# Low parts behind the next slice's products, and weight roundings that start three slices later, in a gated mixing stage

## The chip, the cores and the metric

The kernel runs on one core of a Trainium2 chip. A core has five engines that run side by side: TensorE (matmuls into PSUM; PE in the profile), VectorE (DVE), ScalarE (ACT), GpSimd (POOL) and SyncE (SP, which here only issues transfers). The metric is the device time of one execution in microseconds (us). Matmuls are done in three passes of rounded operands: each fp32 operand is split into a high part (rounded to the matmul's format, `fp32r`) and a low part (what the rounding left), and high x high, high x low and low x high are summed.

## The reference

Three blocks run one after the other on 4 batches of 768 tokens, 384 features:

```
attn:  per head a delta-rule scan over 768 tokens; its output is x
moe:   h = gelu(x @ w_in);  u, v = halves of h (512 features each)
       v_n = layernorm(v) * g_ln
       v_s = einsum('ts,bsd->btd', w_sg, v_n) + b_sg      # mixing over the tokens
       x   = x + (u * v_s) @ w_out                        # gate, projection
moe2:  xk, xr = two mixes of x with x of the token before
       out = sigmoid(xr @ w_r) * (relu(xk @ w_k)**2 @ w_v)
```

The change lies in the second block's mixing, gate and projection. There the weights w_r and w_v of the third block are also split into their parts, piece by piece, and put into DRAM, to be loaded again for the third block.

## The kernel before, in words

The scan and the first half of the gate unit fill the time to about 360 us. Then comes the stage of the change. It works through eight halves (`halves`, L1037): a half is one batch b and 384 of its tokens (t = 0 or 1). Each half has four slices d of 128 features; `mix(b, t, d)` (L1046) is one slice, 32 in all, which I number 0 to 31 (slices 0 to 3 are batch 0, t = 0; 4 to 7 batch 0, t = 1, and so on).

One slice: TensorE adds up 18 matmuls in a PSUM bank (`mix_mm`, six chunks of tokens, three passes). VectorE applies the scale and the bias into `w` (L1056, reads the bank) and multiplies with u (L1058). ScalarE rounds `w` to the high part `gh` (L120 by way of `split`, L117), and VectorE takes the low part `gl` = w - gh (L123). `w` has two buffers. When the four slices of a half are there, `project` (L1064) lets TensorE run 36 matmuls with w_out (three output blocks of 12, in the order of the slices), and VectorE adds each block to x (L1072). The projection of a half t = 0 is called after the third slice of the half t = 1 (`PD`); that of a half t = 1 at the start of the next batch, after `begin` has put the first four chunks' matmuls of all four slices of the next batch before it (L1082 to L1084).

The v rows that the matmuls read stand in a ring of tiles `g` (chunk c of batch b): `fetch_v` loads them from DRAM on SP's queue, `to_ring` (L888) splits them: ScalarE rounds, and the low part is VectorE's for chunks 0 and 3 and GpSimd's for the others. Chunks 0 to 2 of the next batch are split after slice d = 1 of the half t = 1, chunks 3 to 5 after d = 3 (L1092 to L1100). `load_u` loads u two halves ahead; three buffers.

The split of a piece of w_r or w_v is a job (`narrow`, L154; eleven jobs: three of w_r, eight of w_v): a load by SP into one of three `raw` buffers, a conversion on ScalarE (L164), four instructions on VectorE (L169, L171, L173, L175), one on GpSimd (L177), then the rounding on ScalarE (L120) and the low part on GpSimd (L123), then a write to DRAM by SP (L202). `side(n)` (L1012) places the next n VectorE instructions of the open jobs at the point where it is called; `starts` (L1010) tells at which slice the three buffers first take a job. Two slices lie between a job's load and its first instruction.

The order on the four computing engines and on SP's queue is the order in which the code calls them in this stage (manual schedule). After the last slice the rest of the jobs is drained (L1101). GpSimd's queue then issues the reload of w_v (L1118) and of w_r (L1145); the third block starts with `shift`, whose work on VectorE and ScalarE a scheduler interleaves.

Of the kernel before, what the change touches and what calls it, by code (L numbers as in the profile page):

```python
# [7 lines left out]
F32 = mybir.dt.float32  # L8
# [3 lines left out]
AF = mybir.ActivationFunctionType  # L12
ALU = mybir.AluOpType
# [48 lines left out]
NRAW = 3  # L62
NNA = 2
PD = 2
SD = 1
CS = (5, 4)
VF = (0, 3)
VD = 1
# [18 lines left out]
def fused_kernel(  # L87
# [18 lines left out]
    V, A, G, T = nc.vector, nc.scalar, nc.gpsimd, nc.tensor  # L106
# [10 lines left out]
    def split(eng_hi, eng_lo, src, hi, lo):  # L117

        if eng_hi is A:
            A.activation(hi, src, AF.Copy)  # L120
        else:
            eng_hi.tensor_scalar(hi, src, 1.0, None, op0=ALU.mult)
        eng_lo.tensor_tensor(lo, src, hi.bitcast(F32), op=ALU.subtract)  # L123
# [831 lines left out]
    def mix_mm(pt, b, t, d, c):  # L955
        ds_ = slice(d * P, d * P + P)
        vh, vl = ring[b, c]
        wh, wl = wsl[t][c]
        for i, (v, w) in enumerate(((vh, wh), (vh, wl), (vl, wh))):
            T.matmul(pt[:, :DM], lhsT=v[:, ds_], rhs=w, start=(c == 0 and i == 0),  # L960
                     stop=(c == 5 and i == 2))
# [45 lines left out]
    wr_dh, wr_dl, j2 = scratch(w_r, "wr", 3, DM, DM, st)  # L1007
    wv_dh, wv_dl, j3 = scratch(w_v, "wv", 8, DM, DM, st)
    jobs += j2 + j3
    live, turns, starts = [], [0], [1 + 2 * i for i in range(NRAW)]  # L1010

    def side(n):  # L1012

        while n > 0:
            while jobs and any(x <= turns[0] for x in starts):
                starts.remove(next(x for x in starts if x <= turns[0]))
                j = jobs.pop(0)()
                next(j)
                live.append([turns[0] + 2, j, None])
            e = next((e for e in live if e[0] <= turns[0]), None)  # L1020
            if e is None:
                return
            if e[2]:
                e[2]()
            e[2] = None
            c = next(e[1], None)
            if c is None:
                live.remove(e)
                starts.append(turns[0] + 1)
            elif isinstance(c, tuple) and c[0]:  # L1030
                e[0], e[2] = turns[0] + 1, c[1]
            elif isinstance(c, tuple):
                c[1]()
            else:
                n -= 1

    halves = [(b, t) for b in range(B) for t in range(2)]  # L1037
    us, gs = {}, {}
# [7 lines left out]
    def mix(b, t, d):  # L1046
        sl = slice(t * DM, t * DM + DM)
        pt, c0 = begun.pop(d, (None, 0))
        if pt is None:
            pt = ps.tile([P, HF], F32, name="ms")  # L1050
        for c in range(c0, 6):
            mix_mm(pt, b, t, d, c)
        if d == 0:
            gs[b, t] = [mp.tile([P, 4, DM], F32R, name=x) for x in ("gh", "gl")]
        w = vr.tile([P, DM], F32, name="w", bufs=2)
        V.scalar_tensor_tensor(w, pt[:, :DM], g_sb[:, d:d + 1], b_sb[:, sl],  # L1056
                               op0=ALU.mult, op1=ALU.add)
        V.tensor_tensor(w, w, us[b, t][:, d], op=ALU.mult)  # L1058
        side(1)
        split(A, V, w, gs[b, t][0][:, d], gs[b, t][1][:, d])  # L1060
        side(SD)
        turns[0] += 1

# [13 lines left out]
    for k, (b, t) in enumerate(halves):  # L1077
# [7 lines left out]
        for d in range(4):  # L1085
            if (t, d) == VF and b + 1 < B:
                for c in range(3):
                    fetch_v(b + 1, c)
            mix(b, t, d)
            if d == (PD if k < 7 else 3) and t:  # L1090
                project(*halves[k - 1])
            if t == 1 and b + 1 < B:  # L1092
                if d == VD:
                    for c in range(3):
                        load_v(b + 1, c)
                    for c in range(3, 6):
                        fetch_v(b + 1, c)
                if d == 3:
                    for c in range(3, 6):
                        load_v(b + 1, c)  # L1100
# [136 lines left out]
```

## Time and profile before

| | us |
|---|---|
| three runs: median (lowest to highest) | 755.34 (751.11 to 757.25) |
| the profiled execution | 752.32 |
| its span | 750.3 |
| TensorE busy in the span | 690.7 (92%) |
| VectorE busy | 510.8 (68%) |
| ScalarE busy | 368.8 (49%) |
| GpSimd busy | 202.4 (27%) |

The span is what the profiler saw of one execution; 2.0 us of the execution's time lie around it. Busy shares are means over stages that differ. A wait is idle time of an engine, put down to the instruction that ended it. Times in the rows count from the span's start.

### The profile page before, as it was taken

How to read it: one execution, taken by the hardware profiler on the slowest of the kernel's cores; microseconds unless marked ns; L12 is line 12 of the kernel's file. 1: busy time of each engine (PE TensorE's matmuls, PEld its weight loads, DVE VectorE, ACT ScalarE, POOL GpSimd, SP SyncE). 2: the span in 40 equal slices, each digit the busy share in tenths (PEclk: the TensorE clock that was granted, in tenths of full speed). 3: DMA queues.
4: the chain of work that ended last, by engine and by line, in shares of the span. 5: the costliest groups of instructions: out<-in, count | busy, mean ns of one | idle time of the engine just before them, and what ended most of it. 6: DMA issues, size and time to landing. Idle time of an engine off the chain costs nothing.

```text
span 750.3 us, 24940 instructions
## 1 busy us (share of the span) xinstructions
PE 690.7 (92%) x10832; PEld 640.4 (85%) x10832; DVE 510.8 (68%) x1070; ACT 368.8 (49%) x752; POOL 202.4 (27%) x253
## 2 busy tenths in 40 slices
PE   2568789999898999899989999999999999999998
PEld 2536568878776887779989999999999999999997
DVE  6989999878988795632494949489556564563341
ACT  2226656777666666874232313148445454452240
POOL 3033534454445355453133414420000000000000
PEclk9988989999999999999999999999999999999999
DMA  8503542674555565758755454195000000000000
GB/s 249 118 30 84 140 112 81 178 207 139 147 179 152 162 179 169 223 148 240 240 175 190 127 168 148 66 278 141 33 11 21 32 12 22 22 11 31 12 22 32
DMA packets 81549, 88.75 MB, mean 118 GB/s; under 512 B 24704, under 2 KB 64320, under 8 KB 81440
## 3 DMA queue, kind: packets, MB, share of 16 engines
q1 hardware_dynamic: 76384, 77.72, 35.1%
q0 software_dynamic: 5056, 9.44, 4.6%
q8 instruction: 85, 1.39, 0.8%
q14 instruction: 24, 0.20, 0.1%
HBM read 56.60 MB, written 25.82 MB: 110 GB/s over the span
## 4 chain that ended last, share of the span: by engine, by line
PE 73%; DVE 16%; DMA 4%; issue 3%; POOL 1%; SPq 1%; ACT 1%; POOLq 0%; DVEq 0%; ACTq 0%
PE ms L151 38%; PE ms L960 11%; PE ms L687 6%; PE ms L635 5%; DVE sg L355 4%; DVE sg L393 2%; PE ms L563 2%; PE rk L521 2%; PE sps L549 2%; PE ms L456 2%; PE rk L534 1%; PE rk L498 1%; PE ms L333 1%; PE ms L726 1%; DVE Yt L393 1%
## 5 line engine op out<-in xcount | busy, mean ns | idle before, releaser
L177 POOL TENSOR_TENSOR na<-na,raw 128x256 int32<-128x256 int32 (+2 forms) x43 | 36.4, 846 | 121.6 <-DVE na L175 53.5
L151 PE MATMUL ms<-wvh,sl 128*128 128x384 f32 x192 | 64.6, 336 | 0.0
L151 PE MATMUL ms<-wvl,sh 128*128 128x384 f32 x192 | 64.5, 336 | 0.0
L151 PE MATMUL ms<-wvh,sh 128*128 128x384 f32 x192 | 64.5, 336 | 0.0
L151 PE MATMUL ms<-xm_hi,sw0h 128*128 128x384 f32 x192 | 64.2, 335 | 0.0
L151 PE MATMUL ms<-xm_hi,sw0l 128*128 128x384 f32 x192 | 64.2, 334 | 0.0
L151 PE MATMUL ms<-xm_lo,sw0h 128*128 128x384 f32 x192 | 64.2, 334 | 0.0
L120 ACT ACTIVATE gh<-w 128x384 fp32r<-128x384 f32 x32 | 16.8, 525 | 94.9 <-DVE w L1058 94.9
L123 DVE TENSOR_TENSOR sl<-sg,sh 128x384 fp32r<-128x384 f32 x64 | 35.7, 558 | 30.2 <-ACT sh L120 30.2
L960 PE MATMUL ms<-sw0h,g 128*128 128x384 f32 x192 | 50.6, 336 | 3.0 <-ACT g L120 2.1
L120 ACT ACTIVATE sh<-sg 128x384 fp32r<-128x384 f32 x64 | 33.5, 524 | 35.9 <-DVE sg L1157 35.9
L960 PE MATMUL ms<-ws1h,g 128*128 128x384 f32 x192 | 49.9, 334 | 0.0
L355 DVE TENSOR_TENSOR sg<-sg,Yt 128x512 f32<-128x512 f32 (+10 forms) x78 | 46.7, 599 | 1.8
L1173 DVE TENSOR_TENSOR sg<-sg,ms 128x384 f32<-128x384 f32 x24 | 13.3, 554 | 45.3 <-PE ms L151 45.3
L1157 DVE TENSOR_TENSOR sg<-sg 128x384 f32<-128x384 f32 x64 | 35.5, 554 | 10.9 <-ACT sg L1156 10.9
L1156 ACT ACTIVATE sg<-ms 128x384 f32<-128x384 f32 x64 | 30.8, 481 | 23.7 <-PE ms L151 22.9
L514 POOL TENSOR_SCALAR_AFFINE_SELECT SQ<-SQ 64x512 f32<-64x512 f32 x36 | 27.5, 763 | 52.9 <-ACT SQ L513 51.7
L335 PE MATMUL ms<-kT 64*32 64x64 f32 (+1 forms) x640 | 23.3, 235 | 17.9 <-issue 17.9
L687 PE MATMUL ms<-xl,wiu_hi 128*128 128x256 f32 x144 | 39.7, 297 | 0.0
L687 PE MATMUL ms<-xh,wiu_lo 128*128 128x256 f32 x144 | 38.6, 291 | 0.9 <-issue 0.9
L333 PEld LDWEIGHTS ms<-kT 64*32 64x32 f32 x640 | 20.0, 131 | 22.2 <-issue 14.5
L120 ACT ACTIVATE xm_hi<-sg 128x384 fp32r<-128x384 f32 x48 | 23.3, 516 | 31.4 <-PE ms L151 30.5
(246 smaller groups left out, 2237.8 us busy)
## 6 DMA issues: line engine op xcount, KB each, us to landing
u_d<-ug SPq DMA_DIRECT2D x24, 256.0 KB, 3.8
u<-u_d SPq DMA_DIRECT2D x16, 384.0 KB, 4.6
vn_d<-v SPq DMA_DIRECT2D x22, 256.0 KB, 2.8
vk<-in_vk_dram SPq DMA_DIRECT2D x24, 192.0 KB, 4.0
vk<-in_vk_dram SPq DMA_DIRECT2D x12, 384.0 KB, 4.8
out_dram<-sg SPq DMA_DIRECT2D x24, 192.0 KB, 1.9
kT<-in_kt_d_dram SPq DMA_DIRECT2D x8, 512.0 KB, 5.8
SQ<-in_q_d_dram SPq DMA_DIRECT2D x36, 96.0 KB, 4.1
```

The source lines that it names most:

```text
L120: A.activation(hi, src, AF.Copy)
L123: eng_lo.tensor_tensor(lo, src, hi.bitcast(F32), op=ALU.subtract)
L151: T.matmul(pt, lhsT=a, rhs=b, start=(i == 0), stop=(i == n - 1))
L177: G.tensor_tensor(a.bitcast(I32), a.bitcast(I32), w_lo.bitcast(I32), op=ALU.add)
L333: T.matmul(gps[r:r + 32, p, c0:c1], lhsT=t[r:r + 64, u, 0:32], rhs=t[r:r + 64, u, c0:c1], start=True, stop=True)
L355: V.tensor_tensor(tv, vw(a_t, a_off, a_dims), vw(b_t, b_off, b_dims), op=ALU.mult)
L514: G.affine_select(out=pt, in_=pt, pattern=[[0, 8], [1, C]], compare_op=ALU.is_gt, fill=0.0, base=0, channel_multiplier=-1)
L635: T.matmul(vstat[g, b], lhsT=a[:, c], rhs=w[:, c], start=first, stop=last)
L687: T.matmul(vstat["u"][:, 2 * P * d:2 * P * d + 2 * P], lhsT=w[:, c, ds_], rhs=a[:, c].rearrange("p b t -> p (b t)"), start=first, stop=last)
L960: T.matmul(pt[:, :DM], lhsT=v[:, ds_], rhs=w, start=(c == 0 and i == 0), stop=(c == 5 and i == 2))
L1156: A.activation(r, pt[:, :DM], AF.Relu)
L1157: V.tensor_tensor(r, r, r, op=ALU.mult)
```

## The change

Three things. The low part of a slice is no longer taken behind its own rounding but kept in a list (`owing`) and issued after the next slice's product with u; at the fourth slice of a half t = 1 both open low parts are issued. The three `raw` buffers take their first jobs at slices 4, 6 and 8 instead of 1, 3 and 5. And a slice's two job instructions both stand at its end (`SD = 2`); before, one stood ahead of the low part and one behind (at the fourth slice of a half t = 1 a third one comes ahead of the low parts).

```diff
-SD = 1
+SD = 2
...
-    live, turns, starts = [], [0], [1 + 2 * i for i in range(NRAW)]
+    live, turns, starts, owing = [], [0], [4 + 2 * i for i in range(NRAW)], []
...
         V.tensor_tensor(w, w, us[b, t][:, d], op=ALU.mult)
-        side(1)
-        split(A, V, w, gs[b, t][0][:, d], gs[b, t][1][:, d])
+        A.activation(gs[b, t][0][:, d], w, AF.Copy)
+        if owing:
+            owing.pop()()
+        owing.append(lambda h=gs[b, t][0][:, d], l=gs[b, t][1][:, d]: V.tensor_tensor(
+            l, w, h.bitcast(F32), op=ALU.subtract))
+        if t == 1 and d == 3:
+            side(1)
+            owing.pop()()
         side(SD)
         turns[0] += 1
```

In the changed kernel the rounding `gh` has line 1059, the low part `gl` line 1062, and the lines behind them stand 6 higher (the addition to x is L1078). TensorE's order is the same in both.

VectorE before, slices 4 and 5 and what follows them (`na` and `raw` are a job's tiles, `g_7054` chunk 0 of batch 1):

```order
L1056 SCALAR_TENSOR_TENSOR w<-ms,g_sb,b_sb 128x384
L1058 TENSOR_TENSOR w<-w,u 128x384
L173 TENSOR_SCALAR na<-na 128x384
L123 TENSOR_TENSOR gl<-w,gh 128x384
L175 SCALAR_TENSOR_TENSOR na<-raw,na 128x384
L1056 SCALAR_TENSOR_TENSOR w<-ms,g_sb,b_sb 128x384
L1058 TENSOR_TENSOR w<-w,u 128x384
L169 TENSOR_SCALAR na<-raw 128x384
L123 TENSOR_TENSOR gl<-w,gh 128x384
L171 TENSOR_SCALAR na<-na 128x384
L123 TENSOR_TENSOR g_7054<-stw,g_7054 128x512
```

Each low part follows its own slice's product, with a job's instruction between. VectorE in the changed kernel, slices 4 to 6 (`g_7038` is the same chunk 0):

```order
L1056 SCALAR_TENSOR_TENSOR w<-ms,g_sb,b_sb 128x384
L1058 TENSOR_TENSOR w<-w,u 128x384
L1062 TENSOR_TENSOR gl<-w,gh 128x384
L1056 SCALAR_TENSOR_TENSOR w<-ms,g_sb,b_sb 128x384
L1058 TENSOR_TENSOR w<-w,u 128x384
L1062 TENSOR_TENSOR gl<-w,gh 128x384
L123 TENSOR_TENSOR g_7038<-stw,g_7038 128x512
L1056 SCALAR_TENSOR_TENSOR w<-ms,g_sb,b_sb 128x384
L1058 TENSOR_TENSOR w<-w,u 128x384
L1062 TENSOR_TENSOR gl<-w,gh 128x384
L169 TENSOR_SCALAR na<-raw 128x384
```

Each low part is now that of the slice before, and the first job instruction comes in slice 6.

GpSimd's queue at the end of the stage, before (`sw0l` is a part of w_k, `wvh` and `wvl` are those of w_v):

```order
L1109 DMA sw0l_8061<-wk_d 128x1024
L177 TENSOR_TENSOR na<-na,raw 128x384
L123 TENSOR_TENSOR raw<-na,raw 128x384
L1119 DMA wvh<-wv_d 128x8x384
L1119 DMA wvl<-wv_d 128x8x384
L212 DMA wr_hi<-wr_d 128x3x384
L212 DMA wr_lo<-wr_d 128x3x384
```

And in the changed kernel:

```order
L1115 DMA sw0l_8050<-wk_d 128x1024
L177 TENSOR_TENSOR na<-na,raw 128x384
L123 TENSOR_TENSOR raw<-na,raw 128x384
L177 TENSOR_TENSOR na<-na,raw 128x384
L123 TENSOR_TENSOR raw<-na,raw 128x384
L1125 DMA wvh<-wv_d 128x8x384
L1125 DMA wvl<-wv_d 128x8x384
```

Two jobs instead of one now stand between the load of w_k and the reload of w_v.

## Rows read from the trace of the kernel before

**Rows 1.** Waits of TensorE, 330 to 530 us: waiter <- awaited: us, times, longest

```profile
PE ms L960 <- ACT g L120: 2.1, 1, 2.1
PE ms L960 <- DVE g L123: 0.9, 1, 0.9
```

**Rows 2.** Chain of waits, last long piece: start us, us, engine, tile, line, count

```profile
496.14 250.66 PE ms L151 x1440
```

**Rows 3.** Windows, 392 to 396 us: length, busy us of each engine, clock, DMA

```profile
392.00:396.00 4.00, 1.03 (x5) 0.68 (x5) 3.41 (x5) 2.91 (x6) 2.31 (x2) 1.00 0.38 100
```

**Rows 4.** Timeline, TensorE, 377 to 398 us: start us, us, instruction, [idle before]

```profile
377.22 0.44 PE L151 MATMUL ms<-gh,wo_hi 128*128 128x384 f32 x1
...
378.09 0.34 PE L151 MATMUL ms<-gh,wo_lo 128*128 128x384 f32 x1
...
391.70 0.34 PE L960 MATMUL ms<-sw0h,g 128*128 128x384 f32 x1
394.12 0.45 PE L960 MATMUL ms<-sw0h,g 128*128 128x384 f32 x1 [2.08 <-ACT g L120]
...
395.62 0.62 PE L960 MATMUL ms<-sw0h,g 128*128 128x384 f32 x2 [0.88 <-DVE g L123]
...
397.49 0.34 PE L151 MATMUL ms<-gh,wo_hi 128*128 128x384 f32 x1
```

**Rows 5.** Timeline, ScalarE, around 393 us

```profile
393.02 0.52 ACT L120 ACTIVATE gh<-w 128x384 fp32r<-128x384 f32 x1 [6.07 <-DVE w L1058]
393.45 0.61 ACT L120 ACTIVATE g<-stw 128x512 fp32r<-128x512 f32 x1
```

**Rows 6.** Timeline, VectorE, first product with u, and slice 7's start

```profile
368.43 0.56 DVE L1058 TENSOR_TENSOR w<-w,u 128x384 f32<-128x384 f32 x1 [2.96 <-DMA u<-u_d]
...
391.79 0.61 DVE L1056 SCALAR_TENSOR_TENSOR w<-ms,g_sb,b_sb 128x384 f32<-128x384 f32 x1
```

**Rows 7.** Waits of VectorE, 360 to 540 us: us, times, longest

```profile
DVE gl L123 <- ACT gh L120: 12.3, 26, 0.8
```

**Rows 8.** Groups by line, VectorE, 364 to 530 us: busy, mean ns | idle before

```profile
L173 DVE TENSOR_SCALAR na<-na 128x384 uint32<-128x384 uint32 x11 | 6.5, 592 | 0.0
L175 DVE SCALAR_TENSOR_TENSOR na<-raw,na 128x384 uint32<-128x384 uint32 x11 | 6.1, 551 | 0.0
L169 DVE TENSOR_SCALAR na<-raw 128x384 uint32<-128x384 uint32 x11 | 5.6, 509 | 0.0
...
L171 DVE TENSOR_SCALAR na<-na 128x384 f32<-128x384 f32 x11 | 3.9, 353 | 0.0
```

**Rows 9.** Timeline, ScalarE, rounding of slice 31

```profile
501.18 0.53 ACT L120 ACTIVATE gh<-w 128x384 fp32r<-128x384 f32 x1 [2.55 <-DVE w L1058]
```

**Rows 10.** Timeline, GpSimd, last low part and the reloads

```profile
493.86 1.01 POOL L123 TENSOR_TENSOR raw<-na,raw 128x384 fp32r<-128x384 f32 x1 [1.53 <-ACT raw L120]
499.55 0.95 POOL L1119 DMA_DIRECT2D wvh<-wv_d  x1 [4.67 <-DMA wv_d<-raw]
500.49 0.90 POOL L1119 DMA_DIRECT2D wvl<-wv_d  x1
...
509.72 0.77 POOL L212 DMA_DIRECT2D wr_lo<-wr_d  x1
```

**Rows 11.** Transfers: issues, KB each, median us to landing

```profile
wvl<-wv_d POOLq DMA_DIRECT2D x1, 1536.0 KB, 10.6
raw<-in_w_r_dram SPq DMA_DIRECT2D x3, 384.0 KB, 7.8
...
wr_lo<-wr_d POOLq DMA_DIRECT2D x1, 576.0 KB, 5.1
```

**Rows 12.** Instructions by tile, wr_hi: ns, first and last start

```profile
L151 PE MATMUL ms<-wr_hi,xm_hi x72: 334/334/346, 521.2 to 741.9; 128*128 128x384 f32 x72
```

**Rows 13.** Instructions by tile, wvh

```profile
L151 PE MATMUL ms<-wvh,sh x192: 336/336/336, 522.8 to 746.1; 128*128 128x384 f32 x192
```

**Rows 14.** Timeline, VectorE, a low part of the first feed-forward block

```profile
524.95 0.55 DVE L123 TENSOR_TENSOR sl<-sg,sh 128x384 fp32r<-128x384 f32 x1
```

## The prediction

> **What bounds the kernel now.** I read the waits of TensorE first, over the gate unit's mixing and what lies around it (330 to 530 us). TensorE waits there for anything worth naming only twice: 2.1 us for a rounding on ScalarE and 0.9 us for a low part on VectorE, both for tiles `g`, the ring of split v rows [rows 1]. Everything behind it is matmul against matmul: the chain of waits ends in one piece of 250.66 us for 1440 matmuls, 0.174 us each, from 496.14 us to the end [rows 2]. So after 496 us nothing but a new hole in TensorE's work can change the time, and before it only the hole near 392 us is there to be closed.
>
> The windows view shows the hole: from 392 to 396 us TensorE is busy 1.03 of 4 us, at a granted clock of 1.00, so full speed (2.4 GHz) [rows 3]. It costs no clock on either side. TensorE's timeline gives its size: between 391.70 and 397.49 us the trace lists 13 matmuls, which at 0.174 us are 2.26 us; 5.79 us passed, so **3.53 us** are lost. A small one lies before it: the two matmuls from 377.22 to 378.09 us take 0.87 us in place of 0.35, **0.52 us** lost, where the projection of the first half reaches the low part of slice 3 [rows 4]. (I number the 32 calls of `mix` 0 to 31.)
>
> Then who is late. The `g` that TensorE waits for at 394.12 us is chunk 3 of batch 1. ScalarE rounds it at 393.45, directly behind the rounding of slice 7 at 393.02, which had waited for VectorE's product with u [rows 5]. VectorE began slice 7 at 391.79 us, although TensorE's sums for it were there about 6 us earlier (behind 378.09 us come the last 25 of the first projection's 36 matmuls, to 382.4 us, then slice 7's 18: 382.4 + 3.1 = 385.6 us). VectorE had started with the first product with u at 368.43 us, after 2.96 us of waiting for u [rows 6]. So the road is VectorE's 23.4 us from 368.43 to 391.79 us, and the hole is as long as that road is too long.
>
> **The change, part by part.** *Low parts one slice later.* On VectorE the low part of a slice waits for ScalarE's rounding of the same slice: 12.3 us over 26 such waits, 0.47 us each [rows 7]. Behind the next slice's two products the rounding is long done. Six of these waits lie on the road: 6 x 0.47 = 2.8 us off. What gets later is each low part, by about one slice. Its reader is the projection, which comes three slices after a first half's end, so it still finds slice 3's low part early, and the 0.52 us at 377 us go. At a second half's end two low parts come together, and the last of them waits for ScalarE again; behind it in VectorE's queue stands the low part of `g` chunk 3, whose rounding comes later than slice 7's on ScalarE anyway: nothing lost. The two `w` buffers suffice, since a slice's low part stands ahead of the first write of the slice after next.
>
> *First roundings three slices later.* Of the eleven weight jobs (w_r, w_v) two and three quarters ran on the road, now one. Seven instructions of VectorE go off it: twice L169, L171 and L173, once L175, at mean 0.51, 0.35, 0.59 and 0.55 us [rows 8], 3.45 us. ScalarE and GpSimd lose the matching ones, and SP's queue two raw loads that stood between the loads of u and those of v; the v rows come no later for that. Road: 23.4 - 2.8 - 3.45 = 17.1 us, so VectorE could begin slice 7 at 385.5 us; TensorE's sums are there at 385.6. To close the hole it must begin before 389.6 us (391.88, when TensorE wants the tile, less the 2.28 us from slice 7's start to the end of the rounding of `g` [rows 5, 6]). The margin is about 4 us; for the low part, 0.35 us behind on TensorE, it is nearer 3. So the whole hole should go.
>
> *Two at a slice's end* instead of one before and one after the low part: the same instructions, the same rate; later batches hold one or two more of them per half and lose the waits. Their `g` tiles were in time before, and come no later.
>
> **Sum:** 3.53 + 0.52 = 4.05 us less. Not less than 3.0, the two waits that the trace names [rows 1], if the road closes; not more, since TensorE has no other hole behind 330 us [rows 1, 2].
>
> *What is moved to the end.* The last job now has its VectorE part in slices 28 and 29 and its rounding in slice 31, two slices later than before. Its chain: rounding on ScalarE right behind slice 31's, low part on GpSimd, write to DRAM, then the reload of w_v and, in the same queue, w_r. Before, from the last low part on GpSimd to the reload's issue it took 5.69 us, to w_v's arrival 500.49 + 10.6 = 511.1 us, to w_r's 509.72 + 5.1 = 514.8 [rows 10, 11]; TensorE wanted w_r at 521.2 and w_v at 522.8 [rows 12, 13]. Now slice 31's rounding, at 501.18 before [rows 9], comes at 497.2 if it just moves up with TensorE, or at about 493.5 if VectorE keeps up with it (sums at 496.14 - 4.05, two products). Add 1.0 us to GpSimd's low part, 5.7 to the reload, 11.5 to w_v's arrival: 511.7 to 515.4; w_r 3.7 us behind it as before: 515.4 to 519.1, against a need at 521.2 - 4.05 = 517.2 us. So 0 to **1.9 us** may be given back. I take 0, since VectorE has lost the waits that made it late there.
>
> **Rivals.** *A, the reload bites:* the upper end above; 2.1 us less than before remain. For it: the margin is under 2 us. Against: only if VectorE stays 4 us behind TensorE.
>
> *B, VectorE gains nothing by the reordering.* In the last two halves and the start of the third block VectorE now has four instructions of a job more (2.0 us by the means [rows 8]). If the waits that go were not real time, it would come to the last low part `sl` of the first feed-forward block (524.95 + 0.55 = 525.5 before [rows 14]) 2.0 us later against TensorE, which wants it 21 matmuls behind 522.8, at 526.4 us: 1.1 us of a new hole, 2.9 us gained. For the forecast speaks the row of 12.3 us [rows 7]: the waits are idle time of the engine ended by ScalarE. The Trainium skill, "VectorE: DVE Perf Modes", section "The DRAIN you can't avoid", says the opposite of such edits: eight copies with a semaphore after each took as long as eight with one at the end, and what counts is the number of operations. By that rule this rival would hold and the time be 751.1; no row here shows VectorE waiting for itself in that way. On the row the other side of the wait is another engine, so B gets a small chance.
>
> *C, slower.* The last job's raw load stands two slices ahead of VectorE's first instruction on it, as before, but now in slices 26 to 28, where no projection lies between. Two slices are at the quickest 2 x 1.7 = 3.4 us of VectorE (0.61, 0.56 [rows 6] and a low part like the second); the slow raw loads took 7.8 us to land [rows 11]. VectorE, in order, would stand 4.4 us in slice 28, which goes straight into the chain of the last reload: 1.9 + 4.4 = 6.3 us of hole, 2.2 more than is won, 754.5 us on the profile's scale. It decides from a landing of 5.6 us on (3.4 + 4.05 - 1.9). Against it: SP issues the load as soon as the buffer's former job is written out, without waiting for VectorE, and the 7.8 us fell where u and v were being loaded too.
>
> *D, the change does nothing here:* the u rows or the v rows, not VectorE, hold the ring. Against: at 393.45 us ScalarE took `g` straight behind its predecessor, with no wait for a transfer [rows 5].
>
> **The numbers.** The profiled execution took 752.32 us (span 750.3); less 4.05 it is 748.3. It lies 3.0 us under the median of the three runs, 755.34, and inside their spread (751.11 to 757.25). The mean of the four is 754.0, and from that I forecast **750.0 us**. Chances: forecast 0.66, A 0.16 (751.9), B 0.08 (751.1), C 0.04 (754.0 + 2.2 = 756.2), D or something unseen 0.06 (754). The range goes from the lowest run less the whole gain, 751.11 - 4.05 = 747.1, rounded down to 746.5, to the highest less A's remaining 2.1, 755.2. About 1% (7.5 us) is what a measurement of this kernel can tell from no change; the whole hole is 0.54%. So within 1% has 0.87; faster by more needs the scatter of the runs to help, 0.10; slower by more 0.03.
>
> **What would show it.** Right: TensorE busy throughout 388 to 396 us; no wait for `g`; VectorE's first product of slice 7 near 386 us; the waits of VectorE for the rounding `gh` near 2 us in all instead of 12.3; the last piece of the chain beginning near 492 us and still 0.174 us per matmul. Rival A shows as a hole at the first matmul with w_r near 517 us, B as one for `sl` near 522, C as a VectorE wait for raw in slice 28. Wrong: a hole of TensorE anywhere else behind 330 us, or the old one still there with VectorE waiting for u or for ScalarE.

## The result and the profile after

| | us |
|---|---|
| before, median of 15 runs (lowest to highest) | 754.22 (751.11 to 758.31) |
| changed, median of 15 runs (lowest to highest) | **747.63** (743.37 to 752.10) |
| changed, the profiled execution; its span | 747.35; 745.5 |

The ratio is 0.9913, 95% interval [0.9888, 0.9939]: 6.6 us faster (4.6 to 8.4). I had forecast 750.0 in a range of 746.5 to 755.2, with 0.87 on "within 1%".

TensorE's waits from 325 to 530 us, in the profile of the changed kernel (waiter <- awaited: us, times, longest):

```profile
PE ms L563 <- ACT SQ L540: 0.4, 1, 0.4
PE ms L563 <- POOL rs L666: 0.2, 1, 0.2
```

Both waits for `g` [rows 1] are gone; what is left lies ahead of the mixing. A window over the stretch of the old hole shows TensorE busy in all of it (length, busy time of each engine, clock, DMA), where before it had 1.03 of 4 us [rows 3]:

```profile
390.00:400.00 10.00, 10.00 (x59) 10.00 (x58) 2.38 (x6) 0.00 (x0) 0.99 (x2) 1.00 0.32 113
```

The chain of waits, its first piece of mixing and its last piece (start, length, tile, line, count):

```profile
358.40 16.64 PE ms L960 x96
...
491.36 250.66 PE ms L151 x1440
```

The same chain in the kernel before names the first piece of mixing thus:

```profile
359.10 5.18 PE ms L960 x30
```

The last piece is as long as before [rows 2] to 0.01 us and starts 4.78 us earlier. But the mixing itself began 0.70 us earlier, at 358.40 against 359.10 us. So I measure every kernel from the start of the mixing on TensorE to the end of its last matmul, read from these two pieces of its chain: before 496.14 + 250.66 - 359.10 = 387.70 us, changed 491.36 + 250.66 - 358.40 = **383.62 us**, a difference of 4.08. I call this length the *back part*. In the changed kernel TensorE has no gap in it.

VectorE's first product with u and the start of slice 7 (start, length, instruction, [idle before]):

```profile
367.83 0.56 DVE L1058 TENSOR_TENSOR w<-w,u 128x384 f32<-128x384 f32 x1 [3.06 <-DMA u<-u_d]
...
384.59 0.62 DVE L1056 SCALAR_TENSOR_TENSOR w<-ms,g_sb,b_sb 128x384 f32<-128x384 f32 x1 [0.18 <-PE ms L960]
```

VectorE's road between them takes 16.76 us, where it took 23.36 [rows 6], and VectorE now waits 0.18 us for TensorE's sums there, where before it came to them some 6 us late. ScalarE follows:

```profile
385.83 0.53 ACT L1059 ACTIVATE gh<-w 128x384 fp32r<-128x384 f32 x1 [4.79 <-DVE w L1058]
386.27 0.62 ACT L120 ACTIVATE g<-stw 128x512 fp32r<-128x512 f32 x1
```

`g` is rounded at 386.89 us, 7.2 us earlier than before [rows 5] (6.5 us, counted from the start of the mixing), and 3.7 us before TensorE wants it, at 390.63 us. (That time is the start of the matmul which stood behind the hole, found by its place in the order: the traces of both kernels have the same 2201 matmuls from the start of the mixing on.) VectorE's 12.3 us of waits for `gh` [rows 7] are gone from the list of its waits altogether.

At the other end, where the last job is moved to, GpSimd and ScalarE:

```profile
496.00 1.29 POOL L123 TENSOR_TENSOR raw<-na,raw 128x384 fp32r<-128x384 f32 x1 [3.52 <-ACT raw L120]
500.17 0.95 POOL L1125 DMA_DIRECT2D wvh<-wv_d  x1 [2.88 <-PE ms L151]
501.11 0.89 POOL L1125 DMA_DIRECT2D wvl<-wv_d  x1
504.20 0.74 POOL L212 DMA_DIRECT2D wr_hi<-wr_d  x1 [2.21 <-PE ms L151]
504.94 0.77 POOL L212 DMA_DIRECT2D wr_lo<-wr_d  x1
```

```profile
499.72 1.77 ACT L120 ACTIVATE xm_hi<-sg 128x384 fp32r<-128x384 f32 x4 [3.80 <-DMA wv_d<-raw]
```

And what these transfers took (KB, median us to landing):

```profile
wvl<-wv_d POOLq DMA_DIRECT2D x1, 1536.0 KB, 10.5
wr_hi<-wr_d POOLq DMA_DIRECT2D x1, 576.0 KB, 9.0
wr_lo<-wr_d POOLq DMA_DIRECT2D x1, 576.0 KB, 9.9
```

TensorE's first matmuls with `xm_hi` and with w_r:

```profile
503.92 0.34 PE L151 MATMUL ms<-xm_hi,sw0h 128*128 128x384 f32 x1
...
516.43 0.33 PE L151 MATMUL ms<-wr_hi,xm_hi 128*128 128x384 f32 x1
```

wr_lo is there at 504.94 + 9.9 = 514.8 us, and the first matmul with w_r runs at 516.43: **1.6 us** to spare, where it was 521.2 - (509.72 + 5.1) = 6.4 before [rows 10 to 12]. The row of ScalarE holds something I had not looked for: `xm_hi`, the third block's first rounding, waits 3.80 us until the last job's buffer has been written out, since it takes over memory of the jobs (their pool of tiles is closed and the pool of `xm_hi` opened behind it). Before, it followed directly on slice 31's rounding. TensorE uses it at 503.92 us, so 503.92 - 499.72 - 0.51 = 3.7 us are to spare.

### The profile page after: what moved, and what is told of

Its sections match the earlier page's. It is cut to its first block, busy times and chain, and to the rows that moved or that the text cites. A ratio compares the mean times of both kernels' runs of the same rounds, so it can differ in the third digit from the quotient of the medians.

```text
span 745.5 us, 24942 instructions
## 1 busy us (share of the span) xinstructions
PE 690.3 (93%) x10832; PEld 641.5 (86%) x10832; DVE 514.1 (69%) x1070; ACT 367.9 (49%) x752; POOL 201.6 (27%) x253
## 4 chain that ended last, share of the span: by engine, by line
PE 74%; DVE 17%; issue 3%; ACT 2%; DMA 1%; POOL 1%; SPq 1%; POOLq 0%; DVEq 0%; ACTq 0%
PE ms L151 39%; PE ms L960 13%; PE ms L687 5%; DVE sg L355 5%; PE ms L635 4%; DVE sg L393 3%; PE ms L563 2%; DVE Yt L393 2%; PE rk L521 1%; PE ms L456 1%; PE rk L534 1%; PE sps L549 1%; PE rk L498 1%; PE ms L333 1%; PE ms L726 1%
```

## The experiments

All ratios are to the kernel before, run beside each one on the same chip. The back part is 387.70 us in the first profile of the kernel before. Mixing start and back part are those of each run's profiled execution.

| run | ratio [95%] | mixing starts, us | back part, us |
|---|---|---|---|
| e1 before again | 1.0022 [0.9995, 1.0049] | 358.31 | 388.56 |
| changed | 0.9913 [0.9888, 0.9939] | 358.40 | 383.62 |
| e4 changed again | 0.9927 [0.9900, 0.9955] | 361.40 | 383.62 |
| e2 low parts only | 0.9983 [0.9953, 1.0013] | 357.17 | 388.36 |
| e3 later start only | 0.9893 [0.9866, 0.9921] | 357.83 | 383.62 |
| e7 later start only, again | 0.9936 [0.9907, 0.9965] | 363.26 | 383.62 |
| e5 later work, loads as before | 0.9949 [0.9923, 0.9976] | 358.88 | 383.63 |
| e6 earlier split of `g` | 0.9934 [0.9907, 0.9960] | 358.95 | 383.62 |
| e9 first jobs at 6 | 1.0007 [0.9985, 1.0030] | 359.50 | 386.92 |
| e10 first jobs at 8 | 1.0034 [1.0014, 1.0054] | 355.83 | 389.98 |
| e8 first jobs at 10 | 1.0065 [1.0034, 1.0097] | 358.74 | 393.53 |

**e1, the kernel before once more.** No edit.

> The kernel before, unchanged, for a second profiled execution. Theory H (the gain is TensorE's hole near 392 us and nothing else): ratio 1.000, the hole (matmuls from chunk 3 of the next batch's ring) again 3 to 4 us, the stretch from the first mixing matmuls behind the last u unit to the end of the program within 0.3 us of 391.4 us. Rival V (the hole varies from execution to execution, and the profiled one had a small one, so that the median of 6.6 us is the mean hole): a hole of another size here, 5 us or more. Rival F (the stage gives 4.2 us, the rest of the 6.6 us comes from the time before it, by chance or not): hole as before, and the time up to the mixing differs by a us or more between executions of the same kernel.

The hole is there again:

```profile
PE ms L960 <- ACT g L120: 2.0, 1, 2.0
PE ms L960 <- DVE g L123: 0.9, 1, 0.9
```

But this time it cost clock as well (window behind the hole; the last but two column is the granted clock):

```profile
396.00:398.00 2.00, 2.00 (x8) 2.00 (x7) 0.00 (x0) 0.00 (x0) 2.00 (x3) 0.50 0.28 111
```

```profile
396.77 7.32 PE ms L151 x36
```

At 0.50 (1.2 GHz) eight matmuls fall into these 2 us where thirteen did before; the projection's 36 take 7.32 us and not 6.36. The matmuls begin 0.32 us apart in place of 0.174 from 395.3 us on, already ahead of the projection, and over the whole stretch that costs some 1.5 us. The large hole itself is 3.4 us, as before (3.5). But the back part, 388.56 us, is only 0.86 us longer than in the first profile, because the small hole at 377 us [rows 4] is missing here. So the kernel before loses 3.5 + 0.6 us in one execution and 3.4 us + 1.5 us of clock in the other, 4.1 to 4.9 us against the changed kernel. The stretch to the end of the program is 750.4 - 358.31 = 392.1 us, outside the 391.4 within 0.3 that I expected.

The rows give a reason for the small hole. ScalarE's first conversion for a job (L164) waits for the job's raw load, and the rounding of slice 3 stands right behind it; so the load's landing decides when slice 3's low part is there. The conversion in the first profile, in this one, and in e6 (below), where the small hole is missing too:

```profile
376.21 0.55 ACT L164 ACTIVATE raw<-raw 128x384 int32<-128x384 uint32 x1 [1.85 <-DMA raw<-in_w_r_dram]
374.77 0.57 ACT L164 ACTIVATE raw<-raw 128x384 int32<-128x384 uint32 x1 [1.49 <-DMA raw<-in_w_r_dram]
375.22 0.56 ACT L164 ACTIVATE raw<-raw 128x384 int32<-128x384 uint32 x1 [1.13 <-DMA raw<-in_w_r_dram]
```

Counted from the start of the mixing these are 17.11, 16.46 and 16.27 us. TensorE wants the low part at 18.24 us; it is there at 18.66, 18.02 and 18.00. This is read from the rows; no run moves the load by itself.

**e2, the low parts alone.**

```diff
-        split(A, V, w, gs[b, t][0][:, d], gs[b, t][1][:, d])
+        A.activation(gs[b, t][0][:, d], w, AF.Copy)
+        if owing:
+            owing.pop()()
+        owing.append(lambda h=gs[b, t][0][:, d], l=gs[b, t][1][:, d]: V.tensor_tensor(
+            l, w, h.bitcast(F32), op=ALU.subtract))
+        if t == 1 and d == 3:
+            owing.pop()()
```

(Against the kernel before; the empty list `owing` is added above. SD stays 1, first jobs at 1, 3, 5.)

> Only the low parts behind the next slice's products; the weight jobs start at slices 1, 3 and 5 as before, one instruction ahead of the low part and one behind. Theory H: VectorE's road loses six waits (2.8 us), it begins slice 7 about 389.0 us on the time axis of before, the rounding of ring chunk 3 is in time, its low part 0 to 0.6 us late; the 0.52 us at the first projection go too: 3.4 to 4.0 us faster than before, ratio 0.995. Rival R (the waits are not real time on VectorE; the number of its operations counts): slice 7 begins at 391.8 us, the hole stays, 0 to 0.5 us faster. Rival P (the hole shrinks in proportion to what is taken off the road): about 1.8 us.

It gained next to nothing: 388.36 us lies between the two executions of the kernel before, and the ratio's interval holds 1. TensorE's waits from 325 to 530 us, and VectorE's first job instruction with the low part behind it:

```profile
PE ms L960 <- DVE g L123: 1.8, 1, 1.8
PE ms L151 <- DVE gl L1063: 0.9, 1, 0.9
```

```profile
373.42 0.36 DVE L169 TENSOR_SCALAR na<-raw 128x384 uint32<-128x384 uint32 x1 [2.68 <-DMA raw<-in_w_r_dram]
373.69 0.55 DVE L1063 TENSOR_TENSOR gl<-w,gh 128x384 fp32r<-128x384 f32 x1
```

VectorE does come sooner to the first job, and stands there 2.68 us for its raw load (issued at 365.83 us, in a stretch in which the DMA engines are nearly full: share 0.99 from 366 to 370 us); the low parts of slice 2 (the second row) and of slice 3 stand behind it. Most of what the six waits gave, this one wait took: slice 7 begins 30.50 us behind the start of the mixing, against 32.69 in the first profile of the kernel before and 32.04 in e1. TensorE now waits not for the rounding of `g` but for its low part, which stands behind two low parts of slices on VectorE. And the clock fell here too (window behind the second hole):

```profile
394.00:396.00 2.00, 2.00 (x8) 2.00 (x8) 0.00 (x0) 0.00 (x0) 1.84 (x2) 0.50 0.20 78
```

Of the 4.7 us over the changed kernel some 3.2 are holes, a little less than the 4.1 and 3.4 us of the kernel before, and 1.6 are matmuls at 1.2 GHz. My expectation of 3.4 to 4.0 us fell; the rival R, that VectorE's waits are no real time and slice 7 comes as late as before, is not what the trace shows either.

**e3, the later start alone.**

```diff
-    live, turns, starts = [], [0], [1 + 2 * i for i in range(NRAW)]
+    live, turns, starts = [], [0], [4 + 2 * i for i in range(NRAW)]
```

> Only the first weight jobs three slices later; low parts directly behind their own rounding as before. Theory H: the road loses seven instructions (3.45 us), slice 7 begins about 388.3 us on the axis of before, no hole at the ring; the low part of slice 3 still comes late at the first projection (0.2 to 0.5 us): 3.5 us faster, ratio 0.995. Rival P (in proportion): about 2.2 us. Rival S (the late jobs cost at the end, and only the saved waits pay for it): a hole of 1 to 2 us at the first matmuls with w_r or w_v, about 2 us faster.

The whole gain, 383.62 us. Its road:

```profile
366.33 0.56 DVE L1058 TENSOR_TENSOR w<-w,u 128x384 f32<-128x384 f32 x1 [2.13 <-DMA u<-u_d]
...
386.06 0.60 DVE L1056 SCALAR_TENSOR_TENSOR w<-ms,g_sb,b_sb 128x384 f32<-128x384 f32 x1
```

19.73 us: without the seven job instructions it is 3.63 shorter than in the first profile of the kernel before, and 3.26 shorter than in e1 (390.35 - 367.36 = 22.99). The 0.2 to 0.5 us at the first projection that I expected to stay are gone as well; no job stands in the first slices now. The changed kernel's 16.76 is 2.97 shorter still, and that is what the deferred low parts take off: VectorE's waits on the road fall from 3.6 us (six, for `gh`) to 0.8 (one for `g`, one for TensorE), and one low part of 0.55 us, that of slice 6, now comes behind slice 7's start. It buys margin, no time: from e3's rounding of `g`

```profile
387.73 0.61 ACT L120 ACTIVATE g<-stw 128x512 fp32r<-128x512 f32 x1
```

to its use at 390.05 us there are 1.7 us, in the changed kernel 3.7, and both have no hole. The ratio, 0.9893, lies below the 0.995 I expected, its interval too; the back part accounts for 0.9935 to 0.9946 (below).

**e4, the changed kernel again.** No edit.

> The changed kernel, unchanged, for a second profiled execution. Theory H: no hole of TensorE behind 337 us, the stretch from the first mixing matmuls behind the last u unit to the end 387.1 us, within 0.3; ratio 0.994 (4.2 of 754 us), with its interval reaching 0.9913. Rival F: the same stretch, and the time up to it differs from the first execution's 358.4 us by as much as the rest of the gain.

The back part is the same to 0.01 us, though this execution's mixing starts 3.0 us later.

**e5, the work later but the loads as before.** VectorE's order is that of e3; on SP's queue the first three raw loads stand where they stood in the kernel before.

```diff
-                live.append([turns[0] + 2, j, None])
+                live.append([turns[0] + (2 if turns[0] > 5 else 5), j, None])
```

> The kernel before with one thing changed: the first raw loads stay at slices 1, 3 and 5, but VectorE's, ScalarE's and GpSimd's work on these three jobs begins three slices later, as in the kernel with the later start. VectorE's order is that of the later start, SP's order that of the kernel before. Theory 1 (it is VectorE's seven job instructions on the road to slice 7 that made the hole): slice 7's first product 28 to 29 us behind the end of the last u unit, no wait of TensorE for g, the stage (from that point to the piece of 250.66 us) 133.0 us, like the later start. Theory 2 (it was the two raw loads on SP's queue in the loaded stretch, which held up u or v rows): a wait for g stays, the stage 135.5 us or more. Ratio to the kernel before: 0.989 to 0.995 by theory 1, 0.997 to 1.0 by theory 2.

383.63 us: it is the jobs' work on the engines, on VectorE's road above all, that made the hole, not the two raw loads in SP's queue. Slice 7 starts 29.05 us behind the start of the mixing, against 32.69 before:

```profile
387.93 0.60 DVE L1056 SCALAR_TENSOR_TENSOR w<-ms,g_sb,b_sb 128x384 f32<-128x384 f32 x1
```

**e6, `g` chunk 3 split one slice earlier.** Nothing is taken off VectorE.

```diff
             mix(b, t, d)
+            if t == 1 and d == PD and b + 1 < B:
+                load_v(b + 1, 3)
...
-                    for c in range(3, 6):
+                    for c in range(4, 6):
                         load_v(b + 1, c)
```

> The kernel before with one thing changed: chunk 3 of the next batch's v rows is split behind slice d = 2 of a half t = 1, ahead of the projection and of slice 7, instead of behind slice 7. VectorE does as much work as before on the road, and 0.6 to 1.4 us more (the low part of g) before slice 7. Theory 1 (only the place of g's rounding behind slice 7 on ScalarE makes the hole; slice 7 itself is late but nobody wants it yet): no wait for g, slice 7's first product at 33 to 34 us behind the last u unit, where the kernel before has 32.7, TensorE's projection still finds slice 7's low part; the 0.5 us at 377 us stay; stage 133.2 to 133.8 us, ratio 0.990 to 0.996. Rival (VectorE's lateness only moves the hole): TensorE then waits 1 to 3 us for the gl of slice 7 at the second projection instead of for g; stage 135 to 137 us, ratio 0.996 to 1.0.

383.62 us again. ScalarE's two roundings, in the order in which they now stand:

```profile
386.39 0.63 ACT L120 ACTIVATE g<-stw 128x512 fp32r<-128x512 f32 x1 [0.70 <-DMA stw<-vn_d]
...
392.59 0.53 ACT L120 ACTIVATE gh<-w 128x384 fp32r<-128x384 f32 x1 [5.11 <-DVE w L1058]
```

Slice 7 is as late as before (its rounding at 392.59, before at 393.02 [rows 5]), and nobody minds: TensorE wants it only in the second projection. So VectorE's lateness was never wanted by TensorE itself; it cost time because the rounding of `g` stood behind it in ScalarE's queue, and its low part behind it on VectorE. The 0.5 us at 377 us, which I expected to stay, went too: as in e1, the first raw load landed early enough (third of the ScalarE rows under e1).

**e7, the later start once more.** No new edit.

> The later start alone once more, the same kernel as before in another set of runs. If the reordering of the low parts only buys margin and no time: stage 132.96 us, ratio 0.990 to 0.995, inside the interval of the whole change run beside it earlier. If the reordering costs something or gives something of its own: a ratio outside of that one's interval, 0.9888 to 0.9955.

Inside the changed kernel's interval, with the same back part: the reordering of the low parts neither gives nor costs time here.

**e8, e10, e9: first jobs still later.** The changed kernel with 10, 8 and 6 for 4 (slices 10, 12, 14 and so on). The edit of e8 against the changed kernel:

```diff
-    live, turns, starts, owing = [], [0], [4 + 2 * i for i in range(NRAW)], []
+    live, turns, starts, owing = [], [0], [10 + 2 * i for i in range(NRAW)], []
```

> The changed kernel with the three buffers' first jobs at slices 10, 12 and 14 instead of 4, 6 and 8. Two of the eleven jobs are then done only behind slice 31, and the reloads of w_r and w_v stand behind them. It tests my rival A: that the last reload sets the start of the third block. In the changed kernel the w_r parts were there 1.6 us before the first matmul with them. Theory 1 (the reload is near the path): the two jobs are 8 instructions of VectorE (about 4 us) and GpSimd's parts, so the reloads come 4 to 8 us later, TensorE waits 2.5 to 6.5 us for w_r or w_v near 520 us; stage to 392 us unchanged, no wait for g; ratio to the kernel before 0.996 to 1.001. Rival (there is more slack than the 1.6 us): a wait under 1 us, ratio 0.989 to 0.995.

TensorE's wait, and ScalarE's rounding that ended it:

```profile
PE ms L151 <- ACT xm_hi L120: 6.9, 1, 6.9
```

```profile
510.77 1.76 ACT L120 ACTIVATE xm_hi<-sg 128x384 fp32r<-128x384 f32 x4 [3.55 <-DMA wv_d<-raw]
```

The wait was somewhat longer than the 2.5 to 6.5 us I expected, the ratio of 1.0065 lies above my 0.996 to 1.001, and the place was wrong: it is the hand-over of the jobs' memory to `xm_hi`. Here the reload of w_r stands ahead of that of w_v on GpSimd's queue and does not bite. And the back part grew by 9.91 us, not 6.93. The windows behind the wait:

```profile
511.30:514.00 2.70, 2.65 (x7) 2.34 (x8) 2.67 (x6) 2.25 (x5) 1.71 (x2) 0.50 1.24 354
514.00:518.00 4.00, 4.00 (x16) 4.00 (x16) 2.84 (x6) 2.72 (x7) 0.00 (x0) 0.62 1.47 380
```

17 matmuls took 5.79 us (511.35 to 517.14 us) in place of 2.96, 2.8 us more. Of these 2.1 are steps of 0.32 us in place of 0.174 at 1.2 GHz; the other 0.7 lie in the first two steps, which were longer still.

> The changed kernel with first jobs at 8, 10 and 12. The last low part on GpSimd should come 7.3 us later than in the changed kernel, so xm_hi's first rounding 3.6 us later than TensorE wants it: a wait of 3 to 4.5 us for xm_hi near 504 us. Theory 1 (a hole of TensorE costs its length alone, as in the kernel before): ratio to the kernel before 0.996 to 0.999. Rival (behind a hole TensorE runs a stretch at half speed, as it did behind the 6.9 us in the kernel with 10, 12 and 14, where that cost some 2.7 us more): granted clock under 0.7 behind the wait, ratio 0.999 to 1.003.

```profile
505.64 0.44 PE L151 MATMUL ms<-xm_hi,sw0h 128*128 128x384 f32 x1 [4.12 <-ACT xm_hi L120]
506.23 0.66 PE L151 MATMUL ms<-xm_lo,sw0h 128*128 128x384 f32 x1 [0.15 <-DVE xm_lo L123]
```

```profile
507.00:510.00 3.00, 3.00 (x12) 3.00 (x12) 1.94 (x5) 1.67 (x5) 1.04 (x2) 0.55 1.03 253
```

The rival held: 4.3 us of hole and 2.1 us lost behind it (twelve matmuls from 505.64 to 509.82 us, 4.18 us in place of 2.09), 6.36 in all. Of the 2.1 us 1.4 are steps at the lower clock; 0.7 lie in the first two, where TensorE also waits 0.15 us for `xm_lo` (second row). The measured ratio, 1.0034, lies just above the range I gave it.

> The changed kernel with the three buffers' first jobs at slices 6, 8 and 10. The kernel with 10, 12 and 14 waited 6.9 us, but at another place than my rival A said: for the third block's first tile xm_hi, which ScalarE may only write when the last job's buffer has been written out, and not for the reload of w_r. From that kernel's rows GpSimd's last low part should come 2.9 us later than in the changed kernel. Theory 1 (two separate roads: xm_hi has 3.7 us to spare, the reload of w_r 1.6 us): no wait for xm_hi, its first rounding 0.8 us ahead of its use; a wait of 0 to 1.5 us at the first matmuls with w_r near 516.5 us. Ratio to the kernel before 0.992 to 0.997. Rival (the w_r reload has nothing to do with the jobs): no wait at all, the stage and the last 1440 matmuls without a gap, as in the changed kernel.

```profile
520.87 0.44 PE L151 MATMUL ms<-wr_lo,xm_hi 128*128 128x384 f32 x1 [2.22 <-DMA wr_lo<-wr_d]
```

```profile
wvl<-wv_d POOLq DMA_DIRECT2D x1, 1536.0 KB, 10.8
wr_hi<-wr_d POOLq DMA_DIRECT2D x1, 576.0 KB, 11.5
wr_lo<-wr_d POOLq DMA_DIRECT2D x1, 576.0 KB, 13.5
```

Here my rival A is seen at its own place. There are two roads: `xm_hi` is only just late (0.8 us lost in small gaps near 506 us), and wr_lo, which lands 13.5 us behind its issue in place of 9.9, costs 2.4 us. Theory 1 had the right place and too small a price, 0 to 1.5 us, and its ratio of 0.992 to 0.997 was missed. I had counted with a delay of 2.9 us. Against the start of the mixing wvl (issued at 505.68 us) lands 3.8 us later than in the changed kernel, and wr_lo, issued at 507.28 us right behind it, 4.8 us later. Back part 386.92 us; of the 4.1 to 4.9 us 0.8 to 1.6 are left, and the ratio shows none.

## Why the prediction was right, and where it was off

**The hole.** Right in place, and in size for the execution that was read. The sum said 4.05 us (3.53 + 0.52); two profiles of the changed kernel against the first of the kernel before give 4.08. The 3.53 is there in e1 too (3.4). The 0.52 is not: in the execution that was read the first raw load landed late and ScalarE rounded slice 3 late behind it; in e1 neither is so. The sum looked at the place of the low part alone and had no term for that load.

**"It costs no clock on either side."** True of the execution I read, not of the kernel: in e1 the same large hole brought some 1.5 us at 1.2 GHz. One profile could not show that. This term was missing. Against e1 the sum is 0.9 us short: 1.5 us of clock missing, the 0.52 too much. The gain is 4.1 to 4.9 us.

**The road.** I gave 17.1 us and slice 7 at 385.5 to 385.6 us; measured 16.76, and 384.59 us, which on the axis of before (0.70 later) is 385.3. The seven job instructions were 3.45 in the sum, and e3's road is 3.26 to 3.63 shorter than that of the kernel before; the six waits were 2.8 in the sum, against 2.97 between e3 and the changed kernel. But 0.55 of the 2.97 is slice 6's low part, which the sum left on the road, so that the close fit is in part luck. The margin, about 4 us and nearer 3 for the low part, is 3.7 and 3.4 us.

**What each part does.** The sum did not say which of the two terms was needed, only that together they leave 4 us of margin. One is enough (e3), and the other alone is not (e2): most of the waits taken off VectorE's road came back as a wait for a raw load on the same road, and the hole that was left was followed by the lower clock. That the low parts shorten the road by their own amount holds only once the jobs are out of the first slices.

**The tail.** wr_lo at 514.8 us is 515.5 on the axis of before; I had given 515.4 to 519.1, against a need at 517.2 (now 517.1). Taking the lower end was right. But the way there was partly luck: I had w_r 3.7 us behind w_v as in the rows of before [rows 10, 11], without a reason for it; in fact it is issued once TensorE's last projection ends (its row above names TensorE as releaser) and takes 9.9 us in place of 5.1, and it happens to land 3.2 us behind w_v. **Rival A** did not come, but e9 shows how near it was: two slices later 3.3 us of the gain are lost, 2.4 of them to w_r. And I had not seen the second road, by `xm_hi`, which in e8 and e10 is the one that decides.

**Rival B** (nothing gained by the reordering). The Trainium skill, "VectorE: DVE Perf Modes", section "The DRAIN you can't avoid", reports eight copies with a semaphore after each that took as long as eight with one at the end. The section says nothing of a wait for another engine's work, and that is what VectorE's waits are here. Between e3 and the changed kernel the road of VectorE is 2.97 us shorter with the same products and job instructions and one low part (0.55 us) fewer on it, so some 2.4 us of waiting for ScalarE were real time. Yet in the time the reordering is worth nothing (e7), for another reason: the road is already short enough.

**Rival C** (the last job's raw load). The list of VectorE's waits from 360 to 540 us names none for `raw` in the changed kernel. The mechanism is real all the same: in e2 VectorE stood 2.68 us for the first job's load, and in the kernel before ScalarE stood 1.85 us for it.

**Rival D** (the u or v rows hold the ring). Excluded: e5 leaves the first raw loads, and with them the order of the u and v loads, where they were, moves the jobs' work on the engines, and the hole closes.

**The size.** Measured 6.6 us (4.6 to 8.4) in the first comparison, 5.5 (3.4 to 7.5) in e4, against 4.1 to 4.9 in the traces. The forecast time, 750.0, is 2.4 us above the measured one, about the same surplus. It is not in the back part: all six executions without a hole (of four kernels) have the same 383.62 us to 0.01, while the ratios go from 0.9893 to 0.9949. What scatters is when the mixing starts, 355.83 to 363.26 us over twelve executions, though the change touches nothing ahead of it; within one kernel it is 358.31 and 359.10 before, 358.40 and 361.40 changed, 357.83 and 363.26 with the later start alone. The back part's own 4.1 to 4.9 us are a ratio of 0.9935 to 0.9946, inside the intervals of e4, e5, e6 and e7, at the upper end of the first comparison's and outside e3's. I take the gain to be that, and the surplus to be the front's scatter; it is not shown that the front has no part of its own in it. No kernel of this set can beat the changed one behind the start of the mixing, since TensorE has no gap left there.

## What to carry to other kernels

A late engine costs time only where somebody waits for it, and that may be a different piece of work queued behind it on a third engine: moving that piece (e6) can be worth as much as making the late engine faster. When work is moved towards the end of a stage, list everything that its end releases, the memory it hands over as well as the data it writes; here one more step of two slices would have given 3.3 us of the gain back. To judge a change of half a per cent, measure from a fixed point inside the trace: the back part agreed to 0.01 us in the six executions without a hole, where whole runs of one kernel scattered by 8.7 (743.37 to 752.10). And take a second profile of the kernel before: its two executions differ by 0.86 us in the back part, with different holes and a different clock.

## What the hardware showed that I had not expected

- A hole of TensorE may or may not be followed by a stretch at 1.2 GHz: the same hole of 3.4 to 3.5 us cost no clock in one execution and some 1.5 us in another. Behind a wait of 1.8 us in e2 it cost 1.6 us, behind 4.1 us in e10 1.4, behind 6.9 us in e8 2.1, and behind the 2.2 us in e9 nothing (granted clock 1.00). So the length of the wait alone does not tell whether the clock falls.
- The same transfer of 576 KB (wr_lo) landed after 5.1, 9.9 and 13.5 us, the longer, the closer it was issued behind the reload of w_v (9.2, 3.8 and 1.6 us behind wvl's issue). Its distance from wvl's landing changed less: 3.7, 3.2 and 4.3 us behind it.
- VectorE's operations between two SBUF tiles grew beside a GpSimd operation here, those that read PSUM did not (L1056 took 0.60 to 0.62 us in all 32 slices). In the changed kernel, where GpSimd splits `g` from 378.33 us for 2.86 us, VectorE has

```profile
378.37 0.61 DVE L1056 SCALAR_TENSOR_TENSOR w<-ms,g_sb,b_sb 128x384 f32<-128x384 f32 x1
379.02 1.02 DVE L1058 TENSOR_TENSOR w<-w,u 128x384 f32<-128x384 f32 x1
379.97 1.65 DVE L1062 TENSOR_TENSOR gl<-w,gh 128x384 fp32r<-128x384 f32 x1
```

where the second and third take 0.56 and 0.55 us elsewhere.
